# Attention backward: six blocks of E per step block moved from TensorE transposes to the DMA transposes of G

## The chip, the core and the metric

The kernel runs on one core of a Trainium2 chip. TensorE (PE) does the matmuls and takes weights through a load of its own (PEld), VectorE is DVE, ScalarE is ACT, GpSimd is POOL, and SyncE (SP) issues most DMAs. The metric is the device time of one execution in microseconds, as a median of runs.

## The reference

A transformer-like layer and its gradients, for one sequence of 2048 rows of 512 values in bf16: the output x + s * g, and the gradients of x and of six weights. s is attention with 32 heads of 16 columns on the normalised x, g a gate from an MLP (512 to 1792 to 512).

```python
def _fwd(x, wqkv, wo, w1, b1, w2, b2):
    xn = _layernorm(x)
    q, k, v = heads(xn @ wqkv)                        # 32 heads of 16
    p = softmax(einsum("bhqd,bhkd->bhqk", q, k) * 16 ** -0.5)
    s = merge(einsum("bhqk,bhkd->bhqd", p, v)) @ wo
    g = silu(gelu(_layernorm(xn) @ w1 + b1) @ w2 + b2)
    return x + s * g
out, vjp = jax.vjp(_fwd, x, wqkv, wo, w1, b1, w2, b2)
grads = vjp(grad_out)
```

## The kernel before, in words

There are three stages: projections and the MLP forward (`Pre`), attention forward and backward in one pass (`attention_core`), and the remaining weight gradients (`Grads.run`). The change is in the second, with a little at its end.

`attention_core` goes over 16 pairs of heads times 4 chunks of 512 queries: 64 blocks (index j). A block has 16 steps, one for each 128 keys (kb); the step number over all blocks is g, 1024 in all. Four steps make a chunk of 512 keys (kc = kb // 4). The work of a step, in words:

- `emit_s` (L1158): the scores of both heads, keys by queries, into s in PSUM, of which there is one buffer. `emit_exp` (L1167): ACT writes E = exp(s) as bf16 into one slot of a ring, `ets`, of NE = 11 slots. A slot holds 8 blocks of 128 x 128: four blocks of queries times two heads; block b is number 2 * (query block) + head.
- `emit_d` (L1180): dP, the product of v and the gradient, into d in PSUM (three buffers).
- `emit_mult` (L1198): DVE multiplies d by E into G, in the tile `gts` (one tile for two steps). GpSimd copies one of the eight blocks of E next to it (L1196), so a tile holds 2 x 9 blocks.
- `emit_dmat` (L1215): once in two steps, SP issues one DMA transpose of the 18 blocks of `gts` into `gk`, queries by keys.
- `emit_x` (L1275, L1278, L1282): PE sums E and G into X over the keys of a block: the output, the row sums and dQ.
- `emit_T` (L1235): PE transposes the other seven blocks of E of the step before into the PSUM tile tT, of which there is one buffer; `emit_cT` (L1251) copies them on ACT to `ek`.
- `emit_z` (L1377): twenty steps later (ZOFF = -20), PE forms one of 16 units of Z (dK and dV) for that block from `gk` and `ek`: four matmuls of 512 columns on four groups of 32 columns of the array, side by side. Units of the first half of the keys fall into steps 4 to 11 of the next block, of the second half into steps 12 to 19. `emit_acc` (L1389, L1391) adds Z to a sum on DVE.

In every block but the first, steps 0 and 5 are "cut": they transpose four of their seven blocks only, because the free half of tT takes the transposes of X in float32 (`emit_XT`, L1309), which are needed to finish the block before (`emit_xt`, `emit_fin`). The six blocks so left out follow one at a time as an eighth transpose in steps 4, 6, 7, 8, 12 and 13 (table `OLDER`, L1239), and DVE copies each to `ek` (`emit_cO`, L1258). E of steps 0 and 5 must be kept for that until step 13.

The order on every engine is written out by hand: the loop over g emits the pieces in a fixed order, and each engine works in that order. On PE a step is d, s, s, d of step g and g + 1, then a unit of Z, X of step g - 1, T of step g - 1, and XT where there is one. On ACT it is exp of step g + 1, then the copy of T of step g - 1:

```python
        emit_cO(g - 2)
        ...
        emit_exp(g + 1)
        emit_z(g + ZOFF)
        ...
        emit_T(g - 1)
        emit_XT(g)
        emit_mult(g)
        ...
        emit_cT(g - 1)
        emit_dmat(g)
```

After the last step, twenty more steps hold the rest of Z, the finish of the last block, and the first rows of the next stage (`tail_open`, `tail_mid`, `emit_so`, `flush_adds`).

## Time and profile before

| what | value |
|---|---|
| median of 3 runs | 2170.04 us (2169.92 to 2173.01) |
| the profiled execution | 2167.79 us |
| its span, first to last instruction | 2165.8 us |
| busy: PE, DVE, ACT, POOL | 2128.1, 1894.6, 1781.9, 872.5 us |
| granted TensorE clock | 0.998 |
| DMA, mean | 213 GB/s |

Times of parts come from the profiled execution. An instruction's row gives its line in the kernel, its engine, the tile that it writes and those that it reads, its shape, and its time. A group row gives "busy us, mean ns of one | idle of the engine just before them, and what ended it". A timeline row begins with the start and the length in us. PE's matmuls overlap, so their lengths don't add up; their starts tell more.

### The profile page before, as it was taken

How to read it: one execution, taken by the hardware profiler on the slowest of the kernel's cores; microseconds unless marked ns; L12 is line 12 of the kernel's file. 1: busy time of each engine (PE TensorE's matmuls, PEld its weight loads, DVE VectorE, ACT ScalarE, POOL GpSimd, SP SyncE). 2: the span in 40 equal slices, each digit the busy share in tenths (PEclk: the TensorE clock that was granted, in tenths of full speed). 3: DMA queues.
4: the chain of work that ended last, by engine and by line, in shares of the span. 5: the costliest groups of instructions: out<-in, count | busy, mean ns of one | idle time of the engine just before them, and what ended most of it. 6: DMA issues, size and time to landing. Idle time of an engine off the chain costs nothing.

```text
span 2165.8 us, 74893 instructions
## 1 busy us (share of the span) xinstructions
PE 2128.1 (98%) x30614; PEld 1169.2 (54%) x30663; DVE 1894.6 (87%) x3520; ACT 1781.9 (82%) x2482; POOL 872.5 (40%) x2412
## 2 busy tenths in 40 slices
PE   7999999999999999999999999999999999999999
PEld 4444555555555555555555555555555555444444
DVE  7677899999999999999999999999999998798647
ACT  5755999999999999999999999999999998784214
POOL 4286434343444444344434344444434343611003
PEclk9999999999999999999999999999999999999999
DMA  7986999999999999999999999999999999999975
GB/s 239 276 281 202 198 204 204 198 204 203 202 205 204 199 203 205 201 201 205 197 205 201 201 206 201 204 199 207 201 200 208 200 209 208 299 261 241 252 208 177
DMA packets 1416601, 461.17 MB, mean 213 GB/s; under 512 B 1329150, under 2 KB 1400446, under 8 KB 1416256
## 3 DMA queue, kind: packets, MB, share of 16 engines
q1 hardware_dynamic: 1401952, 425.44, 99.4%
q0 software_dynamic: 12720, 29.37, 5.0%
q8 instruction: 240, 3.93, 0.8%
q10 hardware_dynamic: 1584, 1.57, 0.2%
q14 instruction: 105, 0.86, 0.1%
HBM read 62.79 MB, written 64.75 MB: 59 GB/s over the span
## 4 chain that ended last, share of the span: by engine, by line
PE 92%; DVE 3%; DMA 2%; ACT 1%; issue 1%; POOL 1%; SPq 0%; DVEq 0%; POOLq 0%; ACTq 0%
PE tT L1235 23%; PE d L1180 15%; PE Z L1377 15%; PE X L1282 6%; PE X L1275 5%; PE X L1278 5%; PE s L1158 3%; PE ps_dw L785 2%; PE ps_m L401 2%; PE ps_h L386 2%; PE ps_dh L918 2%; PE ps_dw L1026 2%; PE ps_qkv L234 1%; PE tT L1309 1%; PE ps_dwkv L870 1%; PE ps_dxa L1070 1%
## 5 line engine op out<-in xcount | busy, mean ns | idle before, releaser
L1198 DVE TENSOR_TENSOR gts<-d,ets 128x512 bf16<-128x512 f32 x2048 | 1301.2, 681 | 21.0 <-ACT ets L1167 4.5
L1167 ACT ACTIVATE ets<-s 128x1024 bf16<-128x1024 f32 x1024 | 1051.5, 1027 | 16.6 <-PE d L1180 4.0
L1251 ACT COPY ek<-tT 128x448 f32<-128x448 f32 (+1 forms) x1024 | 524.7, 512 | 113.4 <-PE tT L1235 28.8
L1235 PE MATMUL tT<-ident_bf,ets 128*128 128x128 bf16 x6790 | 557.9, 221 | 0.0
L1235 PEld LDWEIGHTS <-ets 128*128 128x128 bf16 x6790 | 382.4, 98 | 211.0 <-issue 196.6
L1180 PE MATMUL d<-QDT,KVT 32*128 32x512 bf16 x2048 | 470.8, 384 | 0.0
L1196 POOL COPY gts<-ets 128x128 bf16<-128x128 bf16 x1024 | 280.3, 295 | 386.2 <-ACT ets L1167 384.2
L1158 PE MATMUL s<-QDT,KVT 32*128 32x512 bf16 x2048 | 401.2, 379 | 3.0 <-ACT ets L1167 2.4
L1377 PE MATMUL Z<-gk,W 128*32 128x512 bf16 x2304 | 302.9, 389 | 1.3 <-DVE acc L1391 1.3
L1275 PE MATMUL X<-ets,NAT 128*32 128x256 bf16 x4096 | 289.9, 273 | 0.0
L1278 PE MATMUL X<-ets,Lc 128*32 128x256 bf16 x4096 | 289.7, 273 | 0.0
L1282 PE MATMUL X<-gts,NAT 128*17 128x256 bf16 x4096 | 288.5, 273 | 0.0
L1377 PEld LDWEIGHTS <-W 128*32 128x32 bf16 x4096 | 105.3, 93 | 237.7 <-issue 225.0
L1180 PEld LDWEIGHTS <-KVT 32*128 32x128 bf16 x2048 | 149.7, 90 | 114.3 <-issue 21.5
L1377 PE MATMUL Z<-ek,W 128*32 128x512 bf16 x1792 | 203.5, 389 | 0.0
L1278 PEld LDWEIGHTS <-Lc 128*32 128x32 bf16 x4096 | 109.7, 97 | 109.1
L1258 DVE COPY ek<-tT 128x64 f32<-128x64 f32 x378 | 84.8, 224 | 89.6 <-ACT ek L1251 74.4
L1450 POOL COPY tick<-gts 1x2 bf16<-1x2 bf16 x205 | 35.7, 174 | 313.7 <-DVE gts L1198 313.7
L1158 PEld LDWEIGHTS <-KVT 32*128 32x128 bf16 x2048 | 143.9, 90 | 13.8 <-issue 7.4
L1282 PEld LDWEIGHTS <-NAT 128*17 128x17 bf16 x4096 | 113.6, 91 | 14.2 <-issue 0.6
L1275 PEld LDWEIGHTS <-NAT 128*32 128x32 bf16 x4096 | 108.5, 96 | 4.9 <-issue 4.9
L1338 POOL TENSOR_TENSOR W<-NATQq,rL 128x128 bf16<-128x128 bf16 x64 | 25.5, 398 | 147.5 <-DVE rL L1337 109.7
(258 smaller groups left out, 2465.2 us busy)
## 6 DMA issues: line engine op xcount, KB each, us to landing
gk<-gts SPq DMA_TRANSPOSE x512, 5.4
H1T_s<-h1r SPq DMA_DIRECT2D x28, 256.0 KB, 3.5
HGT_s<-hgT SPq DMA_DIRECT2D x8, 896.0 KB, 4.6
DH_s<-stg SPq DMA_DIRECT2D x12, 512.0 KB, 3.5
hch<-DH_s SPq DMA_DIRECT2D x12, 512.0 KB, 5.1
gp<-H1T_s SPq DMA_DIRECT2D x9, 512.0 KB, 5.4
out_dram<-ob_w POOLq DMA_DIRECT2D x36, 128.0 KB, 4.1
NAT_s<-NS SPq DMA_DIRECT2D x4, 1056.0 KB, 6.1
```

What stands on the lines that cost most here:

```text
L1158: nc.tensor.matmul(s[:, hj, :], lhsT=op["KVT"][r:r + 32, kb * 128:(kb + 1) * 128], rhs=op["QDT"][r:r + 32, qc * 512:(qc + 1) * 512], start ...
L1167: nc.scalar.activation(out=st_et[g].rearrange("k b h q -> k h b q"), in_=cur["s"][:].rearrange("k h (b q) -> k h b q", b=4), func=ACT.Exp)
L1180: nc.tensor.matmul(d[:], lhsT=op["KVT"][r:r + 32, kb * 128:(kb + 1) * 128], rhs=op["QDT"][r:r + 32, qc * 512:(qc + 1) * 512], start=True, ...
L1196: nc.gpsimd.tensor_copy(out=gts[:, kb % 2, 8, :], in_=st_et[g][:, b // 2, b % 2, :])
L1198: nc.vector.tensor_tensor(out=gts[:, kb % 2, 4 * hj:4 * hj + 4, :], in0=st_d.pop((g, hj))[:].rearrange("k (b q) -> k b q", b=4), in1=st_et ...
L1235: nc.tensor.transpose(tb[:, i - cut(g), :], et[:, b // 2, b % 2, :], ident_bf[:])
L1251: nc.scalar.copy(out=blk[j]["Ek"][kb // 4][:, kb % 4, c:7].rearrange("q i k -> q (i k)").bitcast(f32), in_=st_T[g][:, 0:(7 - c) * 64])
L1258: nc.vector.tensor_copy(out=blk[g // 16]["Ek"][kk // 4][:, kk % 4, i].bitcast(f32), in_=st_T[g][:, 448:512])
L1275: nc.tensor.matmul(X[r:r + 32, 0:256], lhsT=NATt[:, kb, hj, 1:33], rhs=ev, start=(kb == 0), stop=False, skip_group_check=True, tile_positi ...
L1278: nc.tensor.matmul(X[r:r + 32, 256:512], lhsT=Lc[:], rhs=ev, start=False, stop=False, skip_group_check=True, tile_position=(0, r))
L1282: nc.tensor.matmul(X[r:r + 17, 256:512], lhsT=NATt[:, kb, hj, 0:17], rhs=gv, start=False, stop=(kb == 15), skip_group_check=True, tile_pos ...
L1377: nc.tensor.matmul(Z[r:r + 32, :], lhsT=WT[j % 2][1 - part][:, qb, hj, :], rhs=mv, start=(part == 0 and qb == 0), stop=(part == 1 and qb = ...
```

## The change

The cut steps are 0 and 4 in place of 0 and 5. The six blocks left out there are no longer transposed on PE: in these two steps GpSimd copies four blocks of E beside G in place of one, so that the DMA transpose of that pair of steps carries 21 blocks; the other six transposes of a block still carry 18. The eighth transposes, DVE's copies of them and the table go. Which block of a chunk of keys goes by DMA changes for odd chunks from 0 to 3, so that the blocks of a cut step lie in a row. In Z, the six matmuls whose blocks are now in two places (128 columns in `gk`, 384 in `ek`) are made in two pieces, the second ones after the four first ones. E's ring has 7 slots in place of 11. The finish works in place in xs, and in the tail one of two row buffers (t13) lies in the buffer of xs, its addition being emitted earlier (tail step 6). The second half of a block's finish goes with the cut step (step 5 in place of 6).

```diff
@@ -579,7 +579,7 @@
         return [first] + [lambda c=c: ld(out=self.wo_sb[:, c:c + 1], in_=wov[:, c:c + 1]) for c in (1, 2, 3)] \
             + [lambda i=i: rest[i]() for i in range(6)]
 
-    def tail_open(self, ps_t, ps_s, ps_d):
+    def tail_open(self, ps_t, ps_s, ps_d, xsp):
         free = [(ps_t, "tT"), (ps_s, "s")]
 
         def pT(shape, dt, name):
@@ -598,8 +598,9 @@
         self.cnt = {n: 0 for n in self.rows}
         for i in range(2):
             self.row("oT")
-        for i in range(2):
-            self.row("t13")
+        self.row("t13")
+        self.cnt["t13"] = 0
+        self.rows["t13"][1] = (xsp, "xs", [128, D], f32)
         for i in range(2):
             self.row("ot")
         self.emit_oT(0)
@@ -652,6 +653,8 @@
         if n == 3:
             self.emit_so(1)
             self.emit_oT(3)
+        if n == 6:
+            self.flush_adds()
 
     def run(self):
         nc, k, tc, ctx = self.nc, self.k, self.tc, self.ctx
@@ -675,6 +678,8 @@
         gp = {1: slot("gp1", [128, FC, 512], "gp1"), 0: slot("gp0", [128, FC, 512], "gp0")}
         for i in range(3):
             slot(f"ob{i}", [128, D], f"ob{i}")
+        slot("t131", [128, D], "t131", f32)
+        self.rows["t13"][1] = (slots, "t131", [128, D], f32)
         db1acc = slot("db1acc", [128, FC, 4], "db1acc", f32)
         db1f = slot("db1f", [128, FC], "db1f", f32)
         lns = [slot(f"lns{i}", [128, 4], f"lns{i}", f32) for i in range(4)]
@@ -1113,7 +1118,7 @@
     Lc = k.Lc
     OP = [k.op0, make_op(nc, opnd, 1)]
     opnd.tile([128, 192], mybir.dt.uint8, name="pad_to_256b")
-    NE = 11
+    NE = 7
     ets = etp.tile([128, NE, 4, 2, 128], bf16, name="ets")
     acc = outp.tile([128, 2, 512], f32, name="acc")
     tick = outp.tile([1, 2], bf16, name="tick")
@@ -1181,6 +1186,15 @@
                          start=True, stop=True, tile_position=(r, 0))
 
 
+    def row0(kb):
+        return 3 + 9 * (kb % 2)
+
+    def by_dma(kc):
+        return 3 if kc % 2 else 7
+
+    def left(g):
+        return 16 <= g < NSTEP and g % 16 in (0, 4)
+
     def emit_mult(g):
         a = a_unit(g)
         if a is None:
@@ -1189,13 +1203,15 @@
             return
         kb = a[1]
         if kb % 2 == 0:
-            cur["gts"] = gtp.tile([128, 2, 9, 128], bf16, name="gts")
+            cur["gts"] = gtp.tile([128, 21, 128], bf16, name="gts")
         gts = cur["gts"]
         st_gt[g] = gts
-        b = 7 * (1 - kb // 4 % 2)
-        nc.gpsimd.tensor_copy(out=gts[:, kb % 2, 8, :], in_=st_et[g][:, b // 2, b % 2, :])
+        r0 = row0(kb)
+        b = by_dma(kb // 4)
+        m = 3 if left(g) else 0
+        nc.gpsimd.tensor_copy(out=gts[:, r0 - m:r0 + 1, :], in_=st_et[g].rearrange("k b h q -> k (b h) q")[:, b - m:b + 1, :])
         for hj in range(2):
-            nc.vector.tensor_tensor(out=gts[:, kb % 2, 4 * hj:4 * hj + 4, :],
+            nc.vector.tensor_tensor(out=gts[:, r0 + 1 + 4 * hj:r0 + 5 + 4 * hj, :],
                                     in0=st_d.pop((g, hj))[:].rearrange("k (b q) -> k b q", b=4),
                                     in1=st_et[g][:, :, hj, :], op=ALU.mult)
             if hj == 0:
@@ -1209,34 +1225,29 @@
         j, kb = a
         kc = kb // 4
         if kb % 4 == 1:
-            blk[j]["Gk"][kc] = gbp.tile([128, 4, 9, 128], bf16, name="gk")
+            blk[j]["Gk"][kc] = gbp.tile([128, 39, 128], bf16, name="gk")
         if kb % 2 == 1:
-            gk = blk[j]["Gk"][kc][:, kb % 4 - 1:kb % 4 + 1]
-            nc.sync.dma_start_transpose(out=gk.rearrange("q r x k -> q (r x) k"), in_=st_gt[g][:].rearrange("k a x q -> k (a x q)"))
-
-    OLDER = {4: (0, 0), 6: (0, 1), 7: (0, 2), 8: (5, 0), 12: (5, 1), 13: (5, 2)}
-
-    def cut(g):
-        return 3 if g >= 16 and g % 16 in (0, 5) else 0
-
-    def older(g):
-        return OLDER.get(g % 16) if 16 <= g < NSTEP else None
+            gk = blk[j]["Gk"][kc]
+            lo = 0 if left(g - 1) else 3
+            out = gk[:, lo:21, :] if kb % 4 == 1 else gk[:, 21:39, :]
+            nc.sync.dma_start_transpose(out=out, in_=st_gt[g][:, lo:21, :].rearrange("k x q -> k (x q)"))
+
+    def own(g):
+        if not left(g):
+            return 0, 7
+        return (0, 4) if by_dma(g % 16 // 4) == 7 else (3, 7)
 
     def emit_T(g):
         a = a_unit(g)
         if a is None:
             return
         kk = a[1] % 4
-        et = st_et[g]
+        et = st_et[g].rearrange("k b h q -> k (b h) q")
         t = ps_t.tile([128, 512], f32, name="tT")
         tb = t[:].bitcast(bf16).rearrange("q (i k) -> q i k", k=128)
-        for i in range(cut(g), 7):
-            b = i + a[1] // 4 % 2
-            nc.tensor.transpose(tb[:, i - cut(g), :], et[:, b // 2, b % 2, :], ident_bf[:])
-        if older(g):
-            kk2, i = older(g)
-            b = i + kk2 // 4 % 2
-            nc.tensor.transpose(tb[:, 7, :], st_et[g // 16 * 16 + kk2][:, b // 2, b % 2, :], ident_bf[:])
+        i0, i1 = own(g)
+        for i in range(i0, i1):
+            nc.tensor.transpose(tb[:, i - i0, :], et[:, i + (i >= by_dma(a[1] // 4)), :], ident_bf[:])
         st_T[g] = t
         if kk == 0:
             cur["ek"] = ekc.tile([128, 4, 7, 128], bf16, name="ek")
@@ -1247,15 +1258,9 @@
         if a is None:
             return
         j, kb = a
-        c = cut(g)
-        nc.scalar.copy(out=blk[j]["Ek"][kb // 4][:, kb % 4, c:7].rearrange("q i k -> q (i k)").bitcast(f32),
-                       in_=st_T[g][:, 0:(7 - c) * 64])
-
-    def emit_cO(g):
-        if a_unit(g) is None or not older(g):
-            return
-        kk, i = older(g)
-        nc.vector.tensor_copy(out=blk[g // 16]["Ek"][kk // 4][:, kk % 4, i].bitcast(f32), in_=st_T[g][:, 448:512])
+        i0, i1 = own(g)
+        nc.scalar.copy(out=blk[j]["Ek"][kb // 4][:, kb % 4, i0:i1].rearrange("q i k -> q (i k)").bitcast(f32),
+                       in_=st_T[g][:, 0:(i1 - i0) * 64])
 
     def emit_x(g, part):
         a = a_unit(g)
@@ -1278,7 +1283,8 @@
                 nc.tensor.matmul(X[r:r + 32, 256:512], lhsT=Lc[:], rhs=ev,
                                  start=False, stop=False, skip_group_check=True, tile_position=(0, r))
             else:
-                gv = st_gt[g][:, kb % 2, 4 * hj + half:4 * hj + 4:2, :]
+                r0 = row0(kb) + 1 + 4 * hj
+                gv = st_gt[g][:, r0 + half:r0 + 4:2, :]
                 nc.tensor.matmul(X[r:r + 17, 256:512], lhsT=NATt[:, kb, hj, 0:17], rhs=gv,
                                  start=False, stop=(kb == 15), skip_group_check=True, tile_position=(0, r))
 
@@ -1347,13 +1353,13 @@
         rL, ndl = blk[j].pop("r")
         Ov = Oall[:, st0:st0 + 4, p * 32:(p + 1) * 32].rearrange("q b (h c) -> q b h c", h=2)
         nc.gpsimd.tensor_tensor(out=Ov, in0=XE[:, :, :, 16:32], in1=bc(rL[:]), op=ALU.mult)
-        t1 = finp.tile([128, 4, 2, 16], f32, name="t1")
-        nc.gpsimd.tensor_tensor(out=t1[:], in0=XE[:, :, :, 0:16], in1=bc(ndl[:]), op=ALU.mult)
-        nc.gpsimd.tensor_tensor(out=t1[:], in0=XG[:, :, :, 1:17], in1=t1[:], op=ALU.add)
+        t1 = XE[:, :, :, 0:16]
+        nc.gpsimd.tensor_tensor(out=t1, in0=t1, in1=bc(ndl[:]), op=ALU.mult)
+        nc.gpsimd.tensor_tensor(out=t1, in0=XG[:, :, :, 1:17], in1=t1, op=ALU.add)
         rL4 = finp.tile([128, 4, 2, 1], f32, name="rL4")
         nc.gpsimd.tensor_scalar(out=rL4[:], in0=rL[:], scalar1=0.25, scalar2=None, op0=ALU.mult)
         dQv = dQall[:, st0:st0 + 4, p * 32:(p + 1) * 32].rearrange("q b (h c) -> q b h c", h=2)
-        nc.gpsimd.tensor_tensor(out=dQv, in0=t1[:], in1=bc(rL4[:]), op=ALU.mult)
+        nc.gpsimd.tensor_tensor(out=dQv, in0=t1, in1=bc(rL4[:]), op=ALU.mult)
         blk[j].pop("xs")
 
     def emit_z(g):
@@ -1364,18 +1370,27 @@
         if part == 0 and qb == 0:
             blk[j]["Z"] = ps_z.tile([128, 512], f32, name="Z", tag="z")
         Z = blk[j]["Z"]
+        first, rest = [], []
         for par in range(2):
             kc = 2 * kp + par
+            gk = blk[j]["Gk"][kc]
             for hj in range(2):
-                r = 64 * par + 32 * hj
+                b, bd = 2 * qb + hj, by_dma(kc)
                 if part == 0:
-                    mv = blk[j]["Gk"][kc][:, :, 4 * hj + qb, :]
-                elif 2 * qb + hj == 7 * (1 - par):
-                    mv = blk[j]["Gk"][kc][:, :, 8, :]
+                    first.append((par, hj, 0, gk[:, 4 + 4 * hj + qb:39:9, :]))
+                elif b == bd:
+                    first.append((par, hj, 0, gk[:, 3:39:9, :]))
                 else:
-                    mv = blk[j]["Ek"][kc][:, :, 2 * qb + hj - par, :]
-                nc.tensor.matmul(Z[r:r + 32, :], lhsT=WT[j % 2][1 - part][:, qb, hj, :], rhs=mv,
-                                 start=(part == 0 and qb == 0), stop=(part == 1 and qb == 0), tile_position=(0, r))
+                    ek = blk[j]["Ek"][kc][:, :, b - (b > bd), :]
+                    if left(16 * j + 4 * kc) and bd - 3 <= b < bd:
+                        first.append((par, hj, 0, gk[:, b - bd + 3:b - bd + 4, :]))
+                        rest.append((par, hj, 1, ek[:, 1:4]))
+                    else:
+                        first.append((par, hj, 0, ek))
+        for par, hj, kk, mv in first + rest:
+            r = 64 * par + 32 * hj
+            nc.tensor.matmul(Z[r:r + 32, 128 * kk:128 * (kk + mv.shape[1])], lhsT=WT[j % 2][1 - part][:, qb, hj, :], rhs=mv,
+                             start=(part == 0 and qb == 0), stop=(part == 1 and qb == 0), skip_group_check=True, tile_position=(0, r))
 
     def emit_acc(g):
         u = z_unit(g)
@@ -1397,7 +1412,7 @@
             for b in range(2):
                 nc.gpsimd.dma_start(out=dv[:, kp, b, :], in_=ob[b * 64:(b + 1) * 64, :])
 
-    FIN_AT = {1: 1, 6: 0}
+    FIN_AT = {1: 1, 5: 0}
     FIN_END = {1: 1, 2: 0}
     ZOFF = -20
     late = []
@@ -1419,7 +1434,6 @@
                     L += grads.tail_loads(nc.gpsimd.dma_start)
                 for i, f in enumerate(L):
                     late.append((g + 16 * (i // 4 + (p == 0)) + 6 + 3 * (i % 4), f))
-        emit_cO(g - 2)
         if a_unit(g - 2) is not None:
             emit_xt(g - 1)
             emit_fin(g - 1)
@@ -1447,17 +1461,17 @@
         for it in [x for x in late if x[0] <= g]:
             late.remove(it)
 
-            nc.gpsimd.tensor_copy(out=tick[:], in_=st_gt[g][0:1, kb % 2, 7, 126:128])
+            nc.gpsimd.tensor_copy(out=tick[:], in_=st_gt[g][0:1, row0(kb) + 8, 126:128])
             it[1]()
         if g >= NSTEP:
             grads.tail_mid(g - NSTEP)
         emit_cT(g - 1)
         emit_dmat(g)
         st_gt.pop(g - 3, None)
-        st_et.pop(g - 12, None)
+        st_et.pop(g - 3, None)
         if g == NSTEP:
             ctx_r.close()
-            grads.tail_open(ps_t, ps_s, ps_d)
+            grads.tail_open(ps_t, ps_s, ps_d, xsp)
 
 
 def full_kernel(ctx, tc, A_x, A_wqkv, A_wo, B_x, B_w1, B_b1, B_w2, B_b2, grad_out,
```

## The prediction

> **What bounds the kernel now.** I read the page first, then the attention stage alone, then one block of sixteen steps in the timeline. Of the page, the engine totals and the head of the chain that ended last:
>
> ```profile
> PE 2128.1 (98%) x30614; PEld 1169.2 (54%) x30663; DVE 1894.6 (87%) x3520; ACT 1781.9 (82%) x2482; POOL 872.5 (40%) x2412
> PE 92%; DVE 3%; DMA 2%; ACT 1%; issue 1%; POOL 1%; SPq 0%; DVEq 0%; POOLq 0%; ACTq 0%
> ```
>
> The attention stage lies between about 210 and 1830 us: 1024 steps, some 1.58 us each. The stretches of busy time (columns: stretch, length, then busy us of PE, PEld, DVE, ACT, POOL, the granted clock, DMA share, GB/s) show that in it PE, DVE and ACT are all nearly full:
>
> ```profile
> 220.00:1830.00 1610.00, 1609.65 (x27700) 916.29 (x27699) 1500.62 (x2792) 1484.96 (x2037) 681.13 (x2164) 1.00 1.13 203
> ```
>
> With DVE at 93% and ACT at 92% a busy share doesn't tell which of them sets a step, and PE's 100% includes overlapped matmuls. So I take the start of exp (L1167), once per step on ACT, as the clock. In the timeline of ACT, the last ten steps of block 42 (start us, us):
>
> ```profile
> 1283.44 1.03 ACT L1167 ACTIVATE ets<-s 128x1024 bf16<-128x1024 f32 x1
> ...
> 1291.29 1.03 ACT L1167 ACTIVATE ets<-s 128x1024 bf16<-128x1024 f32 x1
> 1292.39 0.53 ACT L1251 COPY ek<-tT 128x448 f32<-128x448 f32 x1
> 1292.85 1.02 ACT L1167 ACTIVATE ets<-s 128x1024 bf16<-128x1024 f32 x1
> ...
> 1294.40 1.02 ACT L1167 ACTIVATE ets<-s 128x1024 bf16<-128x1024 f32 x1
> ...
> 1295.99 1.03 ACT L1167 ACTIVATE ets<-s 128x1024 bf16<-128x1024 f32 x1
> ...
> 1299.14 1.03 ACT L1167 ACTIVATE ets<-s 128x1024 bf16<-128x1024 f32 x1
> ```
>
> The exps at 1291.29, 1292.85 and 1294.40 are those of steps 11 to 13. Two steps take 3.11 us, 1.555 each: that is the floor, and the timeline of PE over the first of them says why.
>
> ```profile
> 1291.12 0.40 PE L1377 MATMUL Z<-ek,W 128*32 128x512 bf16 x4
> 1291.14 0.10 PEld L1275 LDWEIGHTS <-NAT 128*32 128x32 bf16 x4
> 1291.35 0.28 PE L1275 MATMUL X<-ets,NAT 128*32 128x256 bf16 x4
> 1291.46 0.28 PE L1278 MATMUL X<-ets,Lc 128*32 128x256 bf16 x4
> 1291.57 0.28 PE L1282 MATMUL X<-gts,NAT 128*17 128x256 bf16 x4
> 1291.78 0.56 PE L1235 MATMUL tT<-ident_bf,ets 128*128 128x128 bf16 x7
> 1292.28 0.38 PE L1180 MATMUL d<-QDT,KVT 32*128 32x512 bf16 x1
> 1292.38 0.39 PE L1158 MATMUL s<-QDT,KVT 32*128 32x512 bf16 x2
> ```
>
> The exp begun at 1291.29 ends at 1292.32. Only then may the next scores be written (there is one buffer for s): s at 1292.38, 0.39 long, to 1292.77, and the next exp 0.08 later at 1292.85. That loop holds neither the transposes of E nor any DVE work. The second loop goes T (L1235) -> copy of T (L1251) -> exp. T begins at 1291.78, the copy starts 0.61 later, at 1292.39, and the exp after it 0.46 later. In this step it is just inside the floor: d is issued at 1292.28, and s waits 0.10 more for the exp's end. Where T ends later, the second loop takes over:
>
> ```profile
> 1288.63 0.56 PE L1235 MATMUL tT<-ident_bf,ets 128*128 128x128 bf16 x7
> 1289.04 0.22 PE L1239 MATMUL tT<-ident_bf,ets 128*128 128x128 bf16 x1
> 1289.29 0.53 ACT L1251 COPY ek<-tT 128x448 f32<-128x448 f32 x1
> 1289.72 1.03 ACT L1167 ACTIVATE ets<-s 128x1024 bf16<-128x1024 f32 x1
> ```
>
> Here an eighth transpose, one of the six left-out blocks (L1239), follows the seven. The copy starts 0.66 after T began, 0.05 later than above, and the exp follows the copy at 0.43, the closest seen here. So 0.46 - 0.43 = 0.03 us is all that T may be late before exp is late.
>
> **The change, part by part.** *Six transposes on PE and six copies on DVE leave each block but the first.*
>
> ```profile
> L1258 DVE COPY ek<-tT 128x64 f32<-128x64 f32 x378 | 84.8, 224 | 89.6 <-ACT ek L1251 74.4
> L1239 PE MATMUL tT<-ident_bf,ets 128*128 128x128 bf16 x378 | 82.8, 219 | 0.0
> ```
>
> 378 is 6 x 63 blocks. The DVE copies are 84.8 us busy and 89.6 us of waiting before them, and none of it is on the path that sets a step: exp waits for the copy on ACT, not for this one. I price DVE's relief at zero. What counts is the 0.05 us on PE ahead of ACT's copy. In the block shown, ten steps take 1299.14 - 1283.44 = 15.70 us against 10 x 1.555 = 15.55: 0.15 too much. Part of it has another cause and stays: 1294.40 to 1295.99 is 1.59, 0.035 over, where the X matmuls wait for a product queued on DVE behind the accumulation of Z:
>
> ```profile
> 1293.41 0.68 DVE L1391 TENSOR_TENSOR acc<-Z,acc 128x512 f32<-128x512 f32 x1
> 1294.69 0.33 PE L1282 MATMUL X<-gts,NAT 128*17 128x256 bf16 x4
> 1294.96 0.56 PE L1235 MATMUL tT<-ident_bf,ets 128*128 128x128 bf16 x7
> ```
>
> The other 0.115 belongs to the eighth transposes and to the short step that now comes a step earlier. Over 63 blocks: **-7.2 us**. The first six steps of a block I leave as they are: no eighth transpose ends before step 5, and its lateness comes from other work. ACT's two short copies a block remain two.
>
> *The two short steps are 0 and 4, not 0 and 5.* The XT transposes and the second half of the finish go one step ahead with them; same count, same lengths: 0.
>
> *Z in pieces.* Six Z matmuls a block (378 in all) become one of 128 columns and one of 384, the second pieces behind the four first ones, in the four steps 8 to 11. Columns stream at the same rate in pieces: L1275, L1278 and L1282 above start 0.11 apart for 256 columns, 0.43 ns a column, so 128 + 384 is 0.22 as 512 is. New is a second weight load (0.10 by the PEld row). No row of before has two pieces on one column group while the others still stream. Between groups the loads are hidden: L1275's begin at 1291.14 with Z in flight since 1291.12. So the bounds are 0 (nearest: X to X, with no gap for the load), 0.10 (load bare) and 0.16 (the 384 columns wait until all four first ones are through). I take 0.01, as X to X is the nearest row; it fits in the 0.03, so it costs 0.
>
> The Trainium skill ("TensorE: Matmul & The Clock Gate", Part 3, "The mechanism") says that a weight load overlaps matmuls in flight only where its row group differs, and all of these use all rows. By that rule the second pieces would stand bare behind the first, and the sum would be the 2203 of the slower rival below; the loads of L1275 at 1291.14 go against it as far as they bear.
>
> *DMA and GpSimd.* Two of eight transposes a block carry 21 blocks for 18: 150 for 144, 4.2% more. DMA looks full on the page, but its share counts overlapping packets. Half-microsecond stretches show the spare:
>
> ```profile
> 1290.00:1290.50 0.50, 0.50 (x18) 0.30 (x7) 0.50 (x2) 0.50 (x1) 0.08 (x1) 1.00 0.06 8
> 1291.50:1292.00 0.50, 0.50 (x20) 0.28 (x9) 0.50 (x2) 0.50 (x1) 0.44 (x2) 1.00 1.28 291
> L1215 SPq DMA_TRANSPOSE gk<-gts x512: 1813/2504/4649, 219.2 to 1832.0; - x171
> DMA to landing us min/median/max: 3.8/5.4/7.4
> ```
>
> 8 to 291 GB/s with a mean of 203; 4.2% more is 212. On SP's queue an issue takes at least 1.81 us, x 21/18 = 2.11, within the 3.1 us of two steps. It lands in some 6 us, and Z reads a block of keys twelve or more steps (19 us) later. Cost 0; without that cover, 4.2% of 1610 us = 68 us, excluded by the idle stretch. On GpSimd 126 copies grow from one block to four:
>
> ```profile
> L1196 POOL COPY gts<-ets 128x128 bf16<-128x128 bf16 x1024 | 280.3, 295 | 386.2 <-ACT ets L1167 384.2
> L247 POOL COPY NS<-nat 128x512 bf16<-128x512 bf16 x32 | 19.6, 637 | 37.7 <-ACT nat L239 36.6 <-DVE nat L241 1.1
> 1289.32 0.76 POOL L1196 COPY gts<-ets 128x128 bf16<-128x128 bf16 x3
> ```
>
> 637 - 295 = 0.34 us x 126 = 43 us on an engine busy 681 of 1610. Behind it stand only SP's transposes and later GpSimd work: 0; uncovered, 43 us. *Ring of seven:* the slowest reader of E is GpSimd, whose copies at times catch up in threes. The first of those at 1289.32 belongs to step 7; its exp, one step after the one at 1283.44, ended near 1283.44 + 1.555 + 1.03 = 1286.03: 3.3 us, two steps late, and a slot comes round after seven. 0.
>
> *Tail.* The second row of x + s*g goes through the xs buffer, and its addition is moved ahead of the cast of dK/dV:
>
> ```profile
> 1838.84 1.16 POOL L643 TENSOR_TENSOR ot<-t,s1x 128x512 bf16<-128x512 f32 x1
> 1840.86 0.61 POOL L1395 CAST ob<-acc 128x512 bf16<-128x512 f32 x1 [0.86 <-DVE acc L1391]
> ```
>
> 1.16 us of addition and a DMA issue go where GpSimd idles 0.86; the result is stored and read much later. 0, with -1 to +1 as its bounds.
>
> **Sum.** -7.2 us. The profiled execution took 2167.79 (span 2165.8, 2.0 around it): 2160.6. The median of the runs shown, 2170.04, is 2.2 above the profiled one, so the forecast for the median is 2170.04 - 7.2 = 2162.8, say **2163**. About 0.2% (4.3 us) is what a measurement of this kernel can tell from no change.
>
> **Rivals.**
> *The saving is spent on Z.* If the second weight load is half or fully bare (0.05 to 0.10), T is late by that in four steps where it was late by 0.05 in three of the same stretch. The second loop spans two steps, so a lateness costs (lateness - 0.03)/2 a step: 4 x 0.035 = 0.14 us a block at 0.10, 8.8 us in all, against 7.2 saved: 2171.6; at 0.05, 2.5 us: 2165.3. For it: no row shows the case. Against: the hidden loads of every group. Smaller savings by another lateness fall here too.
> *Slower: the second pieces wait for all four first ones.* Z is 0.16 longer in four steps. PE spares only the 0.10 between d and s, and the second loop gives (0.16 - 0.03)/2 = 0.065 a step, the larger: 4 x 0.065 x 63 = 16.4 us, less 7.2: +9.2, 2179. With the load bare as well, Z is 0.26 longer, PE's spare is exceeded by 0.16 a step, 40 us, 2203. It decides from a lateness of about 0.09. For it: the second pieces use the same columns as first ones in flight. Against: four column groups stream side by side in every Z and X.
> *The transposes don't get through in time* (DMA or SP): it would show as Z waiting on gk, for which the spare above leaves little; up to +68 us.
> *It doesn't do what it says*: the floor in those ten steps is not 1.555 and the steps stay at 1.57: 2170.
>
> **Chances and range.** Forecast (Z's pieces within 0.03): 0.56, own range 2160 to 2165.5 (the tail's 1 us and steps of 0.01 in the readings). Saving spent on Z, or no effect: 0.24, 2165.5 to 2174. Slower by the pieces: 0.17; by the transposes: 0.03. So faster 0.56, same 0.24, slower 0.20. The range reaches from 2159 to 2176: it leaves out most of the slower cases and a little below.
>
> **What would show it.** Right: no DVE copies of 64 columns; exps 1.555 apart from step 6 to 12; one step of about 1.59 at step 13; T to copy 0.61 throughout. Z to X in steps 8 to 11 stays at 0.23 to 0.26. Wrong: Z to X at 0.33 or more there, Z waiting for gk, or steps of 1.57 with the copy on time.

## The result, and the profile after

The kernel after takes 2163.53 us, median of 9 runs (2157.76 to 2168.95), against 2170.04 us before, median of 9 (2168.46 to 2173.06): 0.9963 of before, 95% interval 0.9953 to 0.9973. The profiled execution took 2161.5 us, its span 2159.8, against 2167.79 and 2165.8. The runs lie further apart than before: 11.2 us from lowest to highest, where it was 4.6.

The head of the page after, engine totals and the chain that ended last:

```profile
PE 2120.4 (98%) x30614; PEld 1173.6 (54%) x30663; DVE 1840.7 (85%) x3142; ACT 1782.0 (83%) x2482; POOL 909.5 (42%) x2412
PE 92%; DVE 3%; DMA 2%; ACT 1%; issue 1%; SPq 0%; DVEq 0%; ACTq 0%
```

DVE has lost 378 instructions and 54 us, GpSimd has gained 37 us, and the chain's shares stay where they were. As predicted, totals don't tell what set the steps. The rows of exp of the two kernels, before first (duration min/median/max in ns, then the starts of the first and the last one), cut the span in three:

```profile
L1167 ACT ACTIVATE ets<-s x1024: 1023/1030/1031, 210.9 to 1828.8; 128x1024 bf16<-128x1024 f32 x171
```
```profile
L1172 ACT ACTIVATE ets<-s x1024: 1023/1023/1031, 210.8 to 1819.9; 128x1024 bf16<-128x1024 f32 x171
```

From first to last exp it was 1617.9 us and is 1609.1: **-8.8**. From the last exp to the end of the span it was 2165.8 - 1828.8 = 337.0 and is 339.9: **+2.9**. The sum is the -6.0 of the spans. The timeline of ACT in the block that the prediction looked at (block 42; exps of steps 6, 13, 14 and 16):

```profile
1277.90 1.03 ACT L1172 ACTIVATE ets<-s 128x1024 bf16<-128x1024 f32 x1
...
1288.76 1.02 ACT L1172 ACTIVATE ets<-s 128x1024 bf16<-128x1024 f32 x1
...
1290.34 1.03 ACT L1172 ACTIVATE ets<-s 128x1024 bf16<-128x1024 f32 x1
...
1293.45 1.02 ACT L1172 ACTIVATE ets<-s 128x1024 bf16<-128x1024 f32 x1
```

Ten steps take 15.55 us where they took 15.70, steps 6 to 12 together 10.86, 1.551 each, and step 13, whose cause was to stay, 1.58. Over all blocks but the first two and the last one, the median distance from one exp to the next by its place in the block (place k: from the exp of step k to that of step k + 1), worked out from the starts of all exps (ns; the last column is the sum of the 16, in us; the two kernels in the middle come below):

| place | 3 | 4 | 5 | 7 | 8 | 9 | 10 | 13 | 14 | 15 | the other six | sum |
|---|---|---|---|---|---|---|---|---|---|---|---|---|
| before | 1647 | 1570 | 1644 | 1574 | 1570 | 1573 | 1577 | 1584 | 1560 | 1593 | 1551 to 1558 | 25.219 |
| without the eighth transposes | 1647 | 1583 | 1644 | 1574 | 1552 | 1551 | 1552 | 1580 | 1558 | 1551 | 1551 to 1558 | 25.106 |
| without these and DVE's copies | 1647 | 1584 | 1646 | 1575 | 1552 | 1551 | 1551 | 1579 | 1557 | 1551 | 1551 to 1556 | 25.105 |
| after | 1646 | 1583 | 1644 | 1551 | 1551 | 1552 | 1551 | 1578 | 1558 | 1551 | 1551 to 1558 | 25.079 |

Before to after is -0.140 us a block, -8.8 over 63 blocks: all of what the stage won. PE's timeline over a step with Z whole and one with Z in pieces (a merged row shows the form of its first matmul):

```profile
1280.85 0.40 PE L1392 MATMUL Z<-gk,W 128*32 128x512 bf16 x4
1281.08 0.28 PE L1280 MATMUL X<-ets,NAT 128*32 128x256 bf16 x4
...
1282.40 0.39 PE L1392 MATMUL Z<-gk,W 128*32 128x128 bf16 x2
1282.41 0.39 PE L1392 MATMUL Z<-ek,W 128*32 128x512 bf16 x3
1282.63 0.28 PE L1280 MATMUL X<-ets,NAT 128*32 128x256 bf16 x4
...
1283.06 0.56 PE L1250 MATMUL tT<-ident_bf,ets 128*128 128x128 bf16 x7
```

X begins 0.23 after Z in both. By the trace's nanoseconds the median is 226 for whole units and 229 for steps 8 of all blocks (228 in steps 9, 226 in steps 10 and 11): a unit in pieces costs at most 3 ns. T at 1283.06 has its copy on ACT at 1283.66, 0.60 later.

What the prediction did not say is in three views of after: GpSimd's copies by form, SP's transposes (issue time min/median/max in ns), and the waits in the attention stage:

```profile
L1212 POOL COPY gts<-ets 128x128 bf16<-128x128 bf16 x898 | 253.2, 295 | 301.3 <-ACT ets L1172 283.7 <-DMA gk<-gts 14.7 <-ACT ek L1262 1.8
L1212 POOL COPY gts<-ets 128x512 bf16<-128x512 bf16 x126 | 77.8, 618 | 23.2 <-ACT ets L1172 18.3 <-DMA gk<-gts 4.4
```
```profile
L1233 SPq DMA_TRANSPOSE gk<-gts x512: 1922/2806/4960, 218.9 to 1825.1; - x171
DMA to landing us min/median/max: 3.8/5.8/8.7
```
```profile
POOL gts L1212 <- DMA gk<-gts: 19.1, 15, 2.3
DVE gts L1214 <- DMA gk<-gts: 5.3, 8, 1.0
```

The median issue has gone from 2504 to 2806 ns. GpSimd and DVE now wait at times for a transpose to leave its `gts` tile (of which there are four); the waits of before have no such row. I worked out the true length of an issue, from SP's start or the end of the last product that it reads, whichever is later: 2.70 us in the mean before, 2.95 after, 85% and 93.5% of the time that two steps leave. An issue begins 0.50 and 1.05 us behind its data. Yet in this execution it cost nothing: 10 steps are over their place's median by more than 0.15 us, 2.9 us together; before it was 12 and 3.3.

In the last stage PE's longest wait is the one for dKVn; no other there is over 1.4 us, before or after. The timeline of PE around it, and the stretches behind it (stretch, length, busy us of this line on PE and PEld, the granted clock, DMA share, GB/s), of after:

```profile
1943.62 4.26 PE L875 MATMUL ps_dwkv<-dKVn,xn 128*128 128x512 bf16 x19
1951.64 10.67 PE L875 MATMUL ps_dwkv<-dKVn,xn 128*128 128x512 bf16 x40 [3.75 <-issue]
```
```profile
1951.64:1955.20 3.56, 3.56 (x9) 1.25 (x10) 0.52 0.40 81
1955.20:1960.00 4.80, 4.75 (x23) 2.17 (x23) 1.00 0.55 122
```

and of before (here the busy time of all five engines stands ahead of the clock):

```profile
1959.89 5.34 PE L870 MATMUL ps_dwkv<-dKVn,xn 128*128 128x512 bf16 x23 [2.27 <-issue]
```
```profile
1959.89:1963.40 3.51, 3.50 (x17) 1.62 (x18) 3.37 (x4) 2.13 (x2) 0.00 (x0) 1.00 0.68 118
```

The wait is 3.75 us for 2.27, and behind the longer one the clock was 0.52 for 3.6 us, 9 matmuls in place of 17; behind the shorter it stayed at 1.00. Not all of the longer wait is a loss, because PE came to it earlier. Counted from the start of the last exp, PE stood ready at 128.0 us (1951.64 - 3.75 - 1819.9), before at 128.8; dKVn let it go on at 131.7, before at 131.1. So dKVn is 0.7 us late, the low clock costs 3.56 x 0.48 = 1.7, and what follows these matmuls took 0.6 longer (192.5 for 191.9): but for rounding, the +2.9.

The Trainium skill ("TensorE: Matmul & The Clock Gate", Part 1) says that the array falls to half its clock after an idle window of about 3.4 us and comes back after as long a busy one. These two traces fit that, but the length of a wait alone does not tell what the clock will do, as two later runs show (`a_gts5_4`, then `a_dma_gts5`, both described below; the same line, in `a_gts5_4` at its first matmul):

```profile
1935.80 4.44 PE L875 MATMUL ps_dwkv<-dKVn,xn 128*128 128x512 bf16 x12 [2.13 <-issue]
1935.80:1939.36 3.56, 3.56 (x10) 1.35 (x11) 0.58 1.19 244
```
```profile
2002.86 7.50 PE L875 MATMUL ps_dwkv<-dKVn,xn 128*128 128x512 bf16 x34 [3.51 <-issue]
2002.86:2006.42 3.56, 3.56 (x17) 1.66 (x18) 1.00 1.20 94
```

Behind 2.13 us the clock was down, behind 3.51 us it was not.

### The profile page after: what moved, and what is told of

The parts are those of the page before. It is cut to its first block, busy times and chain, and to the rows that moved or that the text cites. A ratio compares the mean times of both kernels' runs of the same rounds, so it can differ in the third digit from the quotient of the medians.

```text
span 2159.8 us, 74507 instructions
## 1 busy us (share of the span) xinstructions
PE 2120.4 (98%) x30614; PEld 1173.6 (54%) x30663; DVE 1840.7 (85%) x3142; ACT 1782.0 (83%) x2482; POOL 909.5 (42%) x2412
## 3 DMA queue, kind: packets, MB, share of 16 engines
q10 hardware_dynamic: 1584, 1.57, 0.2%
## 4 chain that ended last, share of the span: by engine, by line
PE 92%; DVE 3%; DMA 2%; ACT 1%; issue 1%; SPq 0%; DVEq 0%; ACTq 0%
PE tT L1250 23%; PE d L1185 16%; PE Z L1392 15%; PE X L1288 6%; PE X L1280 5%; PE X L1283 5%; PE s L1163 4%; PE ps_dw L790 2%; PE ps_m L401 2%; PE ps_h L386 2%; PE ps_dh L923 2%; PE ps_dw L1031 2%; PE ps_dwkv L875 1%; PE tT L1315 1%; PE ps_dxa L1075 1%; PE ps_qkv L234 1%
## 5 line engine op out<-in xcount | busy, mean ns | idle before, releaser
L1185 PE MATMUL d<-QDT,KVT 32*128 32x512 bf16 x2048 | 482.8, 384 | 0.1
L1212 POOL COPY gts<-ets 128x128 bf16<-128x128 bf16 (+1 forms) x1024 | 325.3, 335 | 324.4 <-ACT ets L1172 302.0
L1392 PE MATMUL Z<-gk,W 128*32 128x512 bf16 x2682 | 332.4, 367 | 1.1 <-DVE acc L1406 1.1
L1185 PEld LDWEIGHTS <-KVT 32*128 32x128 bf16 x2048 | 161.6, 90 | 114.2 <-issue 21.3
L1392 PE MATMUL Z<-ek,W 128*32 128x512 bf16 (+1 forms) x1792 | 202.7, 376 | 0.0
L1163 PEld LDWEIGHTS <-KVT 32*128 32x128 bf16 x2048 | 155.6, 90 | 13.2 <-issue 7.5
L1280 PEld LDWEIGHTS <-NAT 128*32 128x32 bf16 x4096 | 120.2, 96 | 5.1 <-issue 5.1
L1355 POOL TENSOR_TENSOR Oall<-xs,rL 128x128 bf16<-128x128 f32 x64 | 25.6, 400 | 123.8 <-DVE xs L1323 123.8
## 6 DMA issues: line engine op xcount, KB each, us to landing
out_dram<-ob_w POOLq DMA_DIRECT2D x36, 128.0 KB, 4.1
```

The costliest lines, as they stand in the source:

```text
L1163: nc.tensor.matmul(s[:, hj, :], lhsT=op["KVT"][r:r + 32, kb * 128:(kb + 1) * 128], rhs=op["QDT"][r:r + 32, qc * 512:(qc + 1) * 512], start ...
L1185: nc.tensor.matmul(d[:], lhsT=op["KVT"][r:r + 32, kb * 128:(kb + 1) * 128], rhs=op["QDT"][r:r + 32, qc * 512:(qc + 1) * 512], start=True, ...
L1212: nc.gpsimd.tensor_copy(out=gts[:, r0 - m:r0 + 1, :], in_=st_et[g].rearrange("k b h q -> k (b h) q")[:, b - m:b + 1, :])
L1280: nc.tensor.matmul(X[r:r + 32, 0:256], lhsT=NATt[:, kb, hj, 1:33], rhs=ev, start=(kb == 0), stop=False, skip_group_check=True, tile_positi ...
L1392: nc.tensor.matmul(Z[r:r + 32, 128 * kk:128 * (kk + mv.shape[1])], lhsT=WT[j % 2][1 - part][:, qb, hj, :], rhs=mv, start=(part == 0 and qb ...
```

## The experiments

The theory: the eighth transposes alone make the saving, and what limits the rest is the transposes in SP's queue. The rivals: DVE's relief; a price for Z in pieces; the third stage. Each time is compared with the median of before that was measured with it on the same chip: 2170.74 us for `b_notr`, `b_no8`, `b_nocopy` and `a_zpieces`, 2171.97 for `a_dma`, `a_lag`, `a_dkv` and `a_lag_dkv`, 2171.03 for `b_no8m`, `a_gts5_4` and `a_dma_gts5`, 2170.88 for `b_no8m_tail`. The kernels with a name in b_ leave out transposes or copies that the result needs; they are there for their times. A "long step" is 0.15 us or more over the median of its place.

### What made the saving

**`b_notr`**, the kernel before without the eighth transposes; DVE's copies stay and read a block of the seven.

```diff
-        if older(g):
-            kk2, i = older(g)
-            b = i + kk2 // 4 % 2
-            nc.tensor.transpose(tb[:, 7, :], st_et[g // 16 * 16 + kk2][:, b // 2, b % 2, :], ident_bf[:])
...
-        nc.vector.tensor_copy(out=blk[g // 16]["Ek"][kk // 4][:, kk % 4, i].bitcast(f32), in_=st_T[g][:, 448:512])
+        nc.vector.tensor_copy(out=blk[g // 16]["Ek"][kk // 4][:, kk % 4, i].bitcast(f32), in_=st_T[g][:, 384:448])
```

> The kernel before with the eighth transposes left out and DVE's copies kept (they copy a part of the seven). First theory: nearly the whole saving, 2161 to 2164. Rival (DVE): no saving, 2169 to 2171.

Measured: 2167.01 us, 0.9982 of before (0.9973 to 0.9992). The steps fall as in the table's second row, -0.113 us a block, 7.1 us in all, which is the predicted 7.2. In the profiled execution 15 long steps (6.3 us, before 3.3) and 0.6 us behind the last exp took part of it back. The median, 3.7 us under before, lies between the two expectations: the floor shows nearly the whole saving, the median little more than half of the 6.5 us of the change. The floors account for 1.6 of that difference; the rest is not explained.

**`b_no8`** and **`b_nocopy`**: before without transposes and copies, and without the copies alone. GpSimd puts something else into the six blocks. The part of the edit that both share:

```diff
+        if cut(g):
+            nc.gpsimd.tensor_copy(out=cur["ek"][:, kk, 0:3], in_=et.rearrange("k b h q -> k (b h) q")[:, 0:3, :])
...
-        emit_cO(g - 2)
```

> The kernel before, without the eighth transposes on PE and without their copies on DVE; GpSimd writes something else into those six blocks (it leaves their transposition out, nothing of Z's pieces, the 21-block DMA transposes or the ring is in it). First theory (PE ahead of ACT's copy sets the step): steps 6 to 15 fall to 1.55 but for step 13, attention is 8 to 9 us shorter, as in the changed kernel: 2161 to 2162. Rival (DVE's relief): the same here; the next two tell them apart.

> The kernel before with the eighth transposes kept and only DVE's copies of them left out. First theory: DVE is off the path, so nothing changes: 2169 to 2171, steps 8 to 10 still at about 1.575. Rival (DVE's 85 us and its waits were the price): 6 to 9 us shorter, 2161 to 2164.

Measured: 2174.57 us, 1.0019 (1.0010 to 1.0029), and 2178.08, 1.0036 (1.0024 to 1.0048). Neither tells what it was made for: the new copy reads E, so exp must wait for a further engine at two places in the block. The timeline of ACT of `b_no8`, an ordinary step and then such a one:

```profile
1289.09 1.02 ACT L1167 ACTIVATE ets<-s 128x1024 bf16<-128x1024 f32 x1
1290.19 0.53 ACT L1249 COPY ek<-tT 128x448 f32<-128x448 f32 x1
1290.64 1.02 ACT L1167 ACTIVATE ets<-s 128x1024 bf16<-128x1024 f32 x1
1291.75 0.53 ACT L1249 COPY ek<-tT 128x448 f32<-128x448 f32 x1
1292.28 1.02 ACT L1167 ACTIVATE ets<-s 128x1024 bf16<-128x1024 f32 x1
```

In the ordinary step exp starts 0.45 after the copy, while it still runs; in the other only at its end, 0.53. These two places stand at 1.639 us, 0.087 above the floor; the exps at their ends wait for four semaphores, the others (but for the first uses of a slot) for three. Taken off by hand, `b_no8` would have 25.06 us a block, near after; but that is arithmetic, so it was run again without the artefact. `b_nocopy` was not, and says nothing on DVE's copies.

**`b_no8m`**: as `b_no8`, but GpSimd writes zeros there, which reads nothing. In place of the copy of `b_no8` stands:

```diff
+        if cut(g):
+            nc.gpsimd.memset(cur["ek"][:, kk, 0:3], 0.0)
```

> The kernel before, without the six eighth transposes on PE and without the six copies of 64 columns on DVE; nothing takes the six blocks of E over: GpSimd writes zeros into a few columns of them in their place, so that exp's waits stay those of the kernel before (in the earlier run of this kind they did not). Z stays whole, the DMA transposes carry 18 blocks. Theory (the saving comes from the eighth transposes alone, 0.115 us a block; the new kernel pays some of it back through late DMA transposes): steps 5 to 12 at 1.551 us, steps 10 and 15 not above those of the kernel before, floor 25.06 to 25.10 us a block, time 7 to 9 us under before, 2161 to 2163, which is at or a little under the new kernel. Rival one (the DVE copies matter too): more than 2 us below the run that leaves out the eighth transposes and keeps the copies (0.9982 of before): under 2159. Rival two (the time comes from something else in the change): 2168 to 2171.

Measured: 2167.19 us, 0.9983 (0.9974 to 0.9992). The floor is 25.105 us a block, `b_notr` without the copies has 25.106 with them, and the times agree: DVE's six copies were worth nothing. The time is not the 2161 to 2163 expected. The exps lie 1611.9 us apart, -6.0, but the part behind the last exp is 342.2, +5.2. And the step at place 7 stays at 1575, where the change has 1551. That difference is 0.026 us a block, 1.6 in all. It would fit the short step moved from 5 to 4 and the second half of the finish that moves with it, but no run has that move alone: this cause is argued, not shown.

### Z in pieces, and the transposes

**`a_zpieces`**: the new kernel with all 32 matmuls of Z of the E half in pieces, in place of six.

```diff
-                    first.append((par, hj, 0, gk[:, 3:39:9, :]))
+                    first.append((par, hj, 0, gk[:, 3:12:9, :]))
+                    rest.append((par, hj, 1, gk[:, 12:39:9, :]))
...
-                        first.append((par, hj, 0, ek))
+                        first.append((par, hj, 0, ek[:, 0:1]))
+                        rest.append((par, hj, 1, ek[:, 1:4]))
```

> The changed kernel with every Z matmul of the second half of the units (32 of 64 a block in place of 6) in two pieces of 128 and 384 columns. First theory (the second weight load is hidden): Z to X stays within 0.01 of 0.23, 2162 to 2165. By the rule of the row groups the second pieces stand bare: Z to X 0.33 to 0.49 in eight steps of a block, 20 to 80 us longer, 2183 to 2245.

Measured: 2180.76 us, 1.0059 (1.0033 to 1.0084), and yet not from Z: Z to X is 228 to 229 ns where there are pieces, 226 elsewhere, and the floor is 25.083. The 17 us over after are 36 long steps, 19.7 us, in which the transposes are late. The waits of `a_zpieces`:

```profile
POOL gts L1212 <- DMA gk<-gts: 59.0, 41, 5.9
DVE gts L1214 <- DMA gk<-gts: 26.8, 31, 3.9
```

That the pieces cost PE next to nothing is shown, in this kernel too. Its time is outside both expectations, and why more pieces make the transposes later is not shown: the mean issue grew to 3.03 us with the same 150 blocks.

**`a_dma`**: the new kernel with 21 blocks in four of the eight transposes of a block, 156 blocks for 150. The extra ones are not used.

```diff
-        m = 3 if left(g) else 0
+        m = 3 if kb % 4 == 0 else 0
...
-            lo = 0 if left(g - 1) else 3
+            lo = 0 if kb % 4 == 1 else 3
```

> The changed kernel with 21 blocks in four of eight transposes of a block in place of two (156 blocks for 150) and GpSimd's four-block copy in four steps in place of two: twice the cost that the change put on DMA and GpSimd. First theory (both hidden): 2162 to 2165. Rival (the transposes are the next bound): Z waits for gk or products wait for a free gts; 4% more of DMA's stage time, up to 60 us longer, and if the change's own two already cost something, at least 2 us more here.

Measured: 2213.79 us, 1.0189 (1.0175 to 1.0202). The floor is still 25.087; 70 long steps make 40 us. The waits and the row of the transposes of `a_dma`:

```profile
POOL gts L1212 <- DMA gk<-gts: 99.8, 76, 3.4
DVE gts L1214 <- DMA gk<-gts: 47.2, 56, 2.3
L1233 SPq DMA_TRANSPOSE gk<-gts x512: 1913/2922/5604, 219.5 to 1871.1; - x171
```

The mean issue is 3.12 us, 96% of the two steps, and begins 2.8 us behind its data, GpSimd's copies among them; so it is SP's queue that is late, and not those copies, which have grown as well. So the change stands close before the next bound: the same number of blocks again that it added for nothing costs 48 us (41.8 over before, where after is 6.5 under).

**`a_gts5_4`** and **`a_dma_gts5`**: after and `a_dma` with five `gts` tiles (and E's ring cut to four for the room).

```diff
-    gtp = sbr("gtp", 4)
+    gtp = sbr("gtp", 5)
...
-    NE = 7
+    NE = 4
```

> The new kernel with five tiles gts for the products and copies that the DMA transposes read, in place of four; E's ring is cut from seven steps to four for the room. Theory (single transposes are late and the fourth gts tile is not yet free; their mean rate is still enough): the waits of GpSimd and DVE for a transpose of gk go (19.1 and 5.3 us in the profiled execution), long steps fall from some tens to under ten besides the eight that every kernel has, the time falls by 2 to 5 us to 2158 to 2161 and the runs spread less than 6 us. Rival one (SP's queue is full on the mean, 93.5% of the time): a further tile fills up in its turn, the waits stay within a third of what they were, the time stays at 2162 to 2165. Rival two (E's ring of four is too small, since GpSimd copies at times two steps late): exp waits for GpSimd, ACT shows POOL as what ended its waits at L1167, the time rises above 2166.

> The new kernel with the larger transposes in four of each eight places (21 blocks; 156 blocks a block of queries in place of 150; the run that did this with four tiles gts took 2213.8), and with five tiles gts and E's ring cut to four steps. The three further blocks that are carried are not used. Theory A (throughput: SP's queue is full on the mean): the fifth tile is used up once and the stalls stay: 2205 to 2214. Theory B (single late transposes): with one tile more most of the 70 long steps go, 2165 to 2185. If E's ring of four is what counts, exp waits for GpSimd at L1167 and the time is above 2214.

Measured: 2165.72 us, 0.9973 (0.9961 to 0.9985), and 2211.27, 1.0183 (1.0170 to 1.0196). With the change's 150 blocks the fifth tile takes the waits away in the profiled execution; the one row that is left, and the two of `a_dma_gts5`, in the attention stage:

```profile
DVE gts L1214 <- DMA gk<-gts: 0.2, 1, 0.2
```
```profile
POOL gts L1212 <- DMA gk<-gts: 83.5, 54, 5.1
DVE gts L1214 <- DMA gk<-gts: 47.7, 49, 3.1
```

With 156 blocks the waits stay, 65 long steps, 41.5 us: there it is the mean rate, and a buffer doesn't help. With 150 blocks the median did not fall and the runs still spread over 12 us (2159.84 to 2172.01). My theory that the fourth tile makes the spread falls as far as this shows: the profiled execution was the fastest of the nine, and whether the waits come back in the longer ones was not seen. A ring of four costs nothing either: exp waits 1.3 us in all for GpSimd.

### What is left in a block, and the third stage

**`a_lag`**: the new kernel with X of G one step later, so that PE doesn't wait for a product (places 3, 5 and 13). **`a_dkv`**: other order of SP's loads in the third stage, dKV ahead of H1. **`a_lag_dkv`**: both.

```diff
-        if g % 16 == 2:
+        if 2 <= g % 16 <= 13:
...
-        if g % 16 != 1:
+        if g % 16 in (13, 14, 15, 0):
```
```diff
-                load_h1(3, i)
-            if 1 <= i <= 4:
-                load_dkv(1, i - 1)
+                load_dkv(1, i)
+            if i == 3:
+                for n in range(4):
+                    load_h1(3, n)
```

> The changed kernel with the X matmuls on G two steps behind in steps 2 to 13 in place of one, and the double portion in step 13 in place of step 2. Theory on the steps that stay long (1.64 at step 5, 1.58 at step 13): X waits there for a product queued on DVE behind the accumulation or the copy of X, so T and the copy come late. If so step 5 falls to 1.56 and step 13's excess goes, the 1.64 of step 3 moves to about step 14: 0.09 to 0.11 us a block, 5 to 7 us shorter, 2156 to 2159. Rival (DVE itself is late there): the excess stays, 2163.

> The changed kernel with only the order of SP's loads in the third stage altered: the four transposes of the second half of dK/dV go ahead of the four loads of H1. Theory on the 2.6 us that the profile of the changed kernel is short of attention's 8.9 us: PE reaches these matmuls earlier, waits longer for DMA (4.1 us against 2.7), and its clock then falls to half for some 3.4 us. If so the wait goes and with it the half clock: 3 to 6 us shorter, 2157 to 2161, and the spread of the runs shrinks below 6 us. Rival (the loss is spread over the stage or comes from the moved buffers): less than 1.5 us.

> The two edits before together. If both theories hold the savings add, apart from a longer wait for DMA that the earlier arrival brings: 2151 to 2156. If attention's saving is again lost in the third stage: 2157 to 2160.

Measured: 2165.66 us, 0.9975 (0.9962 to 0.9988); 2163.41, 0.9967 (0.9954 to 0.9979); 2165.49, 0.9970 (0.9958 to 0.9982). With the lag, places 3, 5 and 13 fall to 1551, 1559 and 1551 ns, but 4 rises to 1677, 6 to 1574 and 14 to 1646: the floor is 25.081, as in after. What is won at three places is lost at three others. None of the three kernels came down to the time that was hoped for. The profiled execution of `a_lag` is one of its longest, 2173.82 us, and shows what a long one can look like: 27 long steps, 14.5 us together, with GpSimd waiting 41.7 us and DVE 11.4 us for a transpose (19.1 and 5.3 in the short execution of after). With dKV loaded first, the wait for dKVn and the low clock are gone, and PE waits later. Waits and group rows of `a_dkv`:

```profile
L875 PE MATMUL ps_dwkv<-dKVn,xn 128*128 128x512 bf16 x126 | 27.7, 379 | 0.8 <-ACT ob_w L775 0.7
PE ps_dh L924 <- DVE db1acc L927: 4.5, 3, 2.0
```

The part behind the last exp is 338.1 us, 1.8 less than after; the median does not tell it from after.

**`b_no8m_tail`**: `b_no8m` with the change's tail (row buffer in xs, addition emitted earlier).

```diff
-        for i in range(2):
-            self.row("t13")
+        self.row("t13")
+        self.cnt["t13"] = 0
+        self.rows["t13"][1] = (xsp, "xs", [128, D], f32)
...
+        if n == 6:
+            self.flush_adds()
```

> The kernel before without the six eighth transposes on PE and without the six DVE copies (the six blocks of E are left zero in part, as in the run before this one of that kind, which took 0.9983 of before), and with the new kernel's tail: the second row of x + s*g in the xs buffer and its addition ahead of the cast of dK/dV. Z whole, 18 blocks in the DMA transposes. Theory A (the rest of the new kernel's gain over that run, 0.9963 against 0.9983, is the tail, which the prediction had priced at 0): the product of s*g that waited for its row until 25.3 us after the last exp starts at 23.7, the O transposes end 1.2 to 1.4 us earlier, and the time is 2163 to 2166, 0.996 to 0.9975 of before. Theory B (the third stage is held by its loads, what the tail gives is waited for later): the O transposes end earlier just so, but the end of the weight gradients is not earlier than 337 us after the last exp, time 2167 to 2169. Theory C (the transposes of 21 blocks cost nothing and some other part gave the difference): O transposes not earlier, 2167.

Measured: 2168.35 us, 0.9987 (0.9977 to 0.9996), not better than `b_no8m`. In the new kernel the tail does what was hoped. SP's load of the next rows of x, before, after and in `b_no8m_tail`:

```profile
L569 SPq DMA_DIRECT2D s1x<-in_A_x_dram x1: 373/373/373, 1846.8 to 1846.8; - x1
```
```profile
L569 SPq DMA_DIRECT2D s1x<-in_A_x_dram x1: 372/372/372, 1831.9 to 1831.9; - x1
```
```profile
1829.72 0.46 SPq L569 DMA_DIRECT2D s1b<-in_A_x_dram  x1
1836.09 0.36 SPq L569 DMA_DIRECT2D s1w<-GB_s  x1
...
1838.86 0.58 SPq L569 DMA_DIRECT2D s1x<-in_A_x_dram  x1
```

Counted from the start of the last exp, that load is issued at 18.0 us before the change and at 12.0 after it, because GpSimd's addition, which reads the buffer, comes earlier; the O transposes end 1.4 us sooner (33.5 us behind the end of the last exp, for 34.9). In `b_no8m_tail`, with before's ring, SP stands 6 us ahead of the load of s1w, 5.8 of them by the trace for a matmul of Z, all loads behind come late, and DVE waits for two of them:

```profile
DVE dm_all L630 <- DMA s1b<-GB_s: 2.7, 1, 2.7
DVE dm_all L630 <- DMA s1w<-GB_s: 2.7, 1, 2.7
```

That this comes from where the buffers lie in memory, which the ring's size changes, is argued, not shown. The new kernel without its tail was not run.

## Why the prediction was right, point by point

**The floor, 1.555 us.** Right, 0.004 too high: 1.551 or 1.552 in ten of 16 places.

**Six transposes off PE, -7.2 us.** Right in mechanism, small in size. The floor of `b_notr` gives -7.1 for the transposes alone. Another 1.6 came with the rest of the change, where the prediction had the short step's move in the same 0.115 us: the stage won 8.8. "The first six steps I leave as they are" holds but for step 4, which became 13 ns slower (1570 to 1583). `b_notr` has that too, so it comes with the transposes' going; with five `gts` tiles and a ring of four it is 1572.

**DVE's relief, 0.** Right: `b_no8m` and `b_notr`, without and with DVE's copies, have the same floor and time.

**Z in pieces, 0.01 us.** Right at the lower bound: 0.003, with both rivals on it (0.05 to 0.26 us) excluded. The prediction set against this a sentence of the Trainium skill ("TensorE: Matmul & The Clock Gate", Part 3, "The mechanism"), that a weight load overlaps matmuls in flight only where the row group differs; the same section also lets a load into a background weight buffer go ahead, which the prediction left out. The traces don't bear out the sentence here: with all rows used and other column groups in flight, the load was hidden (229 ns for 226), and `a_zpieces` shows the same for 32.

**DMA and SP, 0.** In the profiled execution the number was right and the reason wrong. The step that failed is "an issue takes at least 1.81 us, x 21/18 = 2.11, within the 3.1": it took the smallest figure of a row whose median, in the same place, was 2.50. By the mean, 2.70, SP's queue was already 85% full, and the change took it to 93.5%. The landing time and Z's twelve steps of spare were not what it hangs on; it is the `gts` tile that is not free for the next products. The rival "transposes don't get through", at 0.03, was much closer than that: `a_dma` shows it 4% further on, at +48 us against after.

**GpSimd, 0.** Right. A copy of four blocks is 618 ns, 0.32 more than one, where 0.34 was estimated, and GpSimd still waits 302 us for exp.

**The ring of seven, 0.** Right in the steps; a ring of four is not felt.

**The tail, 0, -1 to +1.** Wrong in size: its first rows came 1.4 us sooner, of which 0.8 was left when PE came to its wait for dKVn; then the third stage lost more, so that it ends at +2.9 in the profiled execution (dKVn 0.7 late, the clock 1.7, 0.6 behind them). That the change causes this is not shown: over the profiled executions of these kernels the part behind the last exp is between 337 and 347 us, with no order by how fast attention is.

So the forecast of -7.2, for -6.3 in the profiled executions, is two misses that cancel in part: 1.6 too little in the stage, and 2.9 nowhere in the sum. That the number came so close is in part luck. The medians, -6.5 for -7.0, can't be taken apart like this, since one execution of each kernel was profiled; by medians the transposes alone (`b_notr`) bring 3.7 of the 6.5. What the range was mostly made for, Z in pieces, cost nothing, and what it set aside, the transposes, is the next bound.

**Left open.** What brings the median of the change below that of `b_notr`, beyond 1.6 us of floor; why the runs spread more than before (late transposes, as in the long execution of `a_lag`, would do it); why pieces in all of Z make the transposes late; what sets the length of the third stage from one execution to the next.

## What to carry to other kernels

Read a queue's cover from the median or mean of its issue row, not from its minimum, and compare it with the time that is left per issue. Here a queue at 85% took 4% more blocks for nothing in the profiled execution, and the next 4% for 48 us. A DVE that is 93% busy and steps that mostly don't wait for it are no contradiction: find the loop that starts the next step (here scores, exp, scores) and price an edit only by how far it moves that loop. When you take work out to test it, watch that its stand-in adds no wait: a copy in place of a copy made exp wait for one engine more, which hid the whole effect.

## What the runs showed of the hardware

- A second matmul into columns of the same group, with a weight load of its own, behind others in flight: at most 3 ns over an unsplit one (229 for 226), with 6 as with 32 split matmuls a block.
- PE's granted clock was 0.52 for 3.6 us after a wait of 3.75 us, and 1.00 after one of 2.27 us. The length of the wait does not decide it: the clock also fell, for 3.4 us, behind waits of 2.13 (`a_gts5_4`), 2.33 (`b_nocopy`) and 2.66 us (`a_dma`), and stayed at 1.00 behind 3.27 (`b_notr`) and 3.51 us (`a_dma_gts5`). Matmuls of 512 columns stood 427 ns apart at the low clock and 216 at the full one.
- The mean issue of a DMA transpose grew from 2.70 to 2.95 and 3.12 us for 18, 18.75 and 19.5 blocks: 9% and 6% for 4% more each. The count of blocks is not all: with 18 it was 2.77 in `b_no8m`, with 18.75 it was 3.01 in `a_lag` and 3.03 in `a_zpieces`.
- In `b_no8` an exp with a fourth semaphore to wait for, for one more engine, started at the end of the copy before it (0.53 after its start) and not within it (0.45): 0.087 us on the step.
